# Two sequences' q and k loaded as three consecutive tokens per partition in two parts instead of six in one

## The chip, the cores and the metric

The kernel runs on one core of a Trainium2 chip. The metric is the device time of one execution in microseconds (us), the median of several runs. All runs compared here are of the state "fast". The engines are named as the profile names them: PE (TensorE matmuls), PEld (its weight loads), DVE (VectorE), ACT (ScalarE), POOL (GpSimd) and SP (SyncE, which here only issues transfers).

## The reference

Eight sequences of 576 tokens, eight heads of 64, go through causal attention with a window of 128 and a linear distance bias (ALiBi). A block with LayerNorm, a 512 to 2048 to 512 ReLU MLP and a residual follows. Cut to what matters:

```python
scores = q @ k.T / sqrt(64) + bias;  attn = softmax(where(0 <= i - j < 128, scores, -1e9))
x = (attn @ v) as (8, 576, 512);     xn = (x - mean) / sqrt(var + 1e-6) * g_ln
out = x + relu(xn @ w_ch1) @ w_ch2
```

q, k and v are drawn with a standard deviation of 0.1. The scaled products q·k therefore have a spread of about 0.1 x 0.1 x 8 / 8 = 0.01, and the bias decides the softmax almost alone.

## The kernel before

The kernel walks through head pairs of one sequence. For each pair it loads q and k, casts them to fp16, transposes them on PE into a PSUM tile `ptr` (features on partitions, tokens along the row), and copies that tile to SBUF (`qt`, `kt`) for the score matmuls. Sequences 2 to 7 are loaded in runs of 256 bytes (64 floats). Sequences 0 and 1 are needed early, so partition p takes the six consecutive tokens 6p to 6p+5, which makes runs of 1536 bytes. The price is paid after the transposes. Transpose t yields the tokens t, 6+t, 12+t, ..., so the copy out of PSUM must write every sixth fp16 element, 12 bytes apart:

```python
NWIDE = 2; QI = 6; QP = S // QI                       # 96 partitions, 6 tokens each
# load, sequences 0 and 1
out=t[0:QP, :].rearrange("p (h x) -> p h x", h=2),
in_=s.rearrange("h (p i) d -> p h (i d)", i=QI),
...                                                   # cast to c16
for t in range(QI):
    nc.tensor.transpose(ptr[:, t * QP : t * QP + QP], c16[:, t, :, :]..., iden[0:QP, 0:QP])
nc.vector.tensor_copy(                                # line 272
    out=dst[:, 0:S].rearrange("c (p i) -> c i p", i=QI),
    in_=ptr[:, :].rearrange("c (i p) -> c i p", i=QI))
...                                                   # sequences 2 to 7: line 287, dense
nc.vector.tensor_copy(out=dst[:, 0:S], in_=ptr[:, :])
```

After the score matmuls ACT takes the exponential, and DVE multiplies `probs` with the decay mask: line 338 with `mband`, line 347 with `m2g`, a rearranged copy of it. During sequence 0, POOL builds `m2g` and does casts:

```python
def mask_pair(hp):                                    # called once per pair of sequence 0
    nc.gpsimd.tensor_copy(m2g[:, hs, 0:192], mband[:, hs, 0:192])
    nc.gpsimd.tensor_copy(m2g[:, hs, 192:256], mband[:, hs, 0:64])
    nc.gpsimd.tensor_copy(m2g[:, hs, 256:512], mband[:, hs, :])
```

Sequence 0's attention runs alone. Sequence 1's attention runs beside the MLP of the first 512 rows, and so on.

The softmax here doesn't subtract the row's maximum and nothing guards it: scores larger than these inputs give would overflow.

## Time and profile before

| | before |
|---|---|
| median of three runs (range) | 411.57 us (410.92 to 412.39) |
| PE busy, 12 to 41 us (sequence 0) | 11.62 of 29 us |
| PE busy, 110 to 400 us | 286.71 of 290 us |
| one copy of line 272 (12-byte writes), recorded, means of its groups | 2.07 to 2.19 us |
| one copy of line 287 (dense), same 128x576 | 0.458 us |

The first lines are from the profile page of the kernel before: PE's busy share and the granted PE clock in 40 equal slices of the span, in tenths (9 is 90% or more).

```profile
PE   1344497775499999999999999999999999999996
...
PEclk9999998988599999999999999999999999999999
```

The stretches of the same trace have the columns: stretch in us, its length, busy time of PE, PEld, DVE, ACT and POOL (instructions in brackets), granted clock, DMA share, GB/s.

```profile
12.00:41.00 29.00, 11.62 (x138) 8.60 (x138) 21.45 (x30) 9.55 (x15) 12.12 (x20) 1.00 1.15 197
...
62.00:72.00 10.00, 7.55 (x42) 2.72 (x39) 6.21 (x6) 3.84 (x5) 2.14 (x3) 0.83 0.80 181
...
82.00:92.00 10.00, 7.48 (x53) 3.09 (x50) 6.08 (x8) 2.05 (x2) 0.00 (x0) 0.83 0.00 0
...
110.00:400.00 290.00, 286.71 (x2038) 135.91 (x2038) 176.44 (x418) 125.83 (x206) 0.00 (x0) 0.99 0.36 91
```

From 110 us on PE is busy 286.71 of 290 us, so only work before that point can be shortened by this change. Before it PE has gaps.

The groups of instructions of the first 115 us, by shape (line, engine, operation, out<-in, shape, count | busy us, mean ns | idle before), show one group of strided copies and one dense copy:

```profile
L272 DVE COPY kt_115<-ptr 128x576 f16<-128x576 f16 x3 | 6.6, 2193 | 0.0
...
L287 DVE COPY qt_113<-ptr 128x576 f16<-128x576 f16 x1 | 0.5, 458 | 3.0 <-PE ptr L282 3.0
```

The DVE timeline (start us, us, engine, line, operation, out<-in, count, and in brackets the idle time before and its releaser) of sequence 0's first two head pairs, cut to copies and mask multiplies:

```profile
6.69 2.07 DVE L272 COPY qt_111<-ptr 128x576 f16<-128x576 f16 x1 [4.16 <-PE ptr L267]
8.48 2.19 DVE L272 COPY kt_114<-ptr 128x576 f16<-128x576 f16 x1
12.43 0.82 DVE L338 TENSOR_TENSOR probs<-probs,mband 128x1024 f16<-128x1024 f16 x1 [1.76 <-ACT probs L333]
13.48 0.69 DVE L347 TENSOR_TENSOR probs<-probs,m2g 128x1024 f16<-128x1024 f16 x1 [0.22 <-ACT probs L329]
...
21.68 2.07 DVE L272 COPY qt_113<-ptr 128x576 f16<-128x576 f16 x1 [1.72 <-PE ptr L267]
23.47 0.80 DVE L338 TENSOR_TENSOR probs<-probs,mband 128x1024 f16<-128x1024 f16 x1
```

The q and k copies at 6.69 and 8.48 us are back to back and start 1.79 us apart. The q copy at 21.68 us belongs to the next pair. The mask multiply at 23.47 us stands behind it on DVE: its input, an exponential on ACT, was finished at 21.68 us (20.66 + 1.02), but it starts only when the copy is through.

The PE timeline of sequence 1 shows what the copies cost there. In brackets is PE's idle time before the score matmuls:

```profile
66.28 0.49 PE L320 MATMUL sc<-qt_112,kt_115 64*128 64x256 f16 x4 [2.45 <-DVE kt_115 L272]
...
77.83 0.39 PE L320 MATMUL sc<-qt_113,kt_116 64*128 64x256 f16 x4 [2.52 <-DVE kt_116 L272]
...
87.36 0.61 PE L320 MATMUL sc<-qt_111,kt_114 64*128 64x256 f16 x4 [2.52 <-DVE kt_114 L272]
...
88.30 1.91 PE L483 MATMUL pm_771<-w2sb,ht 128*128 128x512 f16 x4
...
98.55 0.39 PE L320 MATMUL sc<-qt_112,kt_115 64*128 64x256 f16 x4 [2.18 <-DVE kt_115 L272]
```

PE waits 2.45, 2.52, 2.52 and 2.18 us for the k copies. The four matmuls of 512 columns at 88.30 us, after one of these waits, take 1.91 us together; the granted clock from 88.30 to 90.20 us is 0.50 (and again 0.50 from 66.71 to 68.96 us, after the first wait).

### The profile page before, as it was taken

How to read it: one execution, taken by the hardware profiler on the slowest of the kernel's cores; microseconds unless marked ns; L12 is line 12 of the kernel's file. 1: busy time of each engine (PE TensorE's matmuls, PEld its weight loads, DVE VectorE, ACT ScalarE, POOL GpSimd, SP SyncE). 2: the span in 40 equal slices, each digit the busy share in tenths (PEclk: the TensorE clock that was granted, in tenths of full speed). 3: DMA queues.
4: the chain of work that ended last, by engine and by line, in shares of the span. 5: the costliest groups of instructions: out<-in, count | busy, mean ns of one | idle time of the engine just before them, and what ended most of it. 6: DMA issues, size and time to landing. Idle time of an engine off the chain costs nothing.

```text
span 410.8 us, 6580 instructions
## 1 busy us (share of the span) xinstructions
PE 352.6 (86%) x2544; PEld 170.6 (42%) x2544; DVE 254.8 (62%) x555; ACT 158.2 (39%) x257; POOL 28.4 (7%) x54
## 2 busy tenths in 40 slices
PE   1344497775499999999999999999999999999996
PEld 0232243323344454445444444444444444444442
DVE  5686936669656776677678576857685768222211
ACT  2341353111356235614651564165326533530510
POOL 4750432000000000000000000000000000000000
PEclk9999998988599999999999999999999999999999
DMA  9999997503624543457345335644421004002002
GB/s 205 199 204 197 235 174 177 114 0 122 149 59 109 128 129 99 94 145 197 85 106 146 115 85 122 152 138 111 113 81 53 0 2 133 29 0 78 26 27 77
DMA packets 110271, 45.30 MB, mean 110 GB/s; under 512 B 97440, under 2 KB 105120, under 8 KB 110240
## 3 DMA queue, kind: packets, MB, share of 16 engines
q1 hardware_dynamic: 105664, 40.36, 40.3%
q0 software_dynamic: 4224, 4.19, 6.4%
q8 instruction: 20, 0.33, 0.3%
q10 hardware_dynamic: 352, 0.33, 0.3%
q14 instruction: 11, 0.09, 0.1%
HBM read 37.26 MB, written 9.44 MB: 114 GB/s over the span
## 4 chain that ended last, share of the span: by engine, by line
PE 57%; DVE 22%; ACT 9%; issue 7%; DMA 3%; SPq 1%; DVEq 0%; ACTq 0%
PE pm L497 21%; PE pm L464 20%; ACT probs L333 6%; DVE probs L347 5%; PE ptr L282 4%; PE ppv L360 3%; PE pxt L425 3%; PE sc L320 2%; ACT ht L472 2%; PE ppv L369 2%; DVE kt_114 L272 2%; DVE st L399 1%; DVE qt_112 L272 1%; DMA v_1_106<-in_v_dram 1%; DMA iden<-iden 1%
## 5 line engine op out<-in xcount | busy, mean ns | idle before, releaser
L497 PE MATMUL pm<-w2sb,ht 128*128 128x512 f16 x512 | 123.4, 379 | 0.0
L472 ACT ACTIVATE ht<-pm 128x512 f16<-128x512 f32 x108 | 64.6, 598 | 83.7 <-PE pm L464 83.7
L333 ACT ACTIVATE probs<-sc 128x1024 f16<-128x1024 f32 x60 | 61.4, 1023 | 90.6 <-PE sc L320 90.6
L464 PEld LDWEIGHTS <-w1sb 128*128 128x128 f16 x576 | 48.8, 99 | 52.5 <-issue 7.5
L497 PEld LDWEIGHTS <-ht 128*128 128x128 f16 x512 | 45.4, 98 | 45.2 <-issue 1.3
L338 DVE TENSOR_TENSOR probs<-probs,mband 128x1024 f16<-128x1024 f16 x32 | 22.5, 703 | 41.5 <-ACT probs L333 41.5
L474 DVE TENSOR_SCALAR ht<-pm 128x512 f16<-128x512 f32 x36 | 24.8, 688 | 33.9 <-PE pm L464 33.9
L360 PEld LDWEIGHTS <-probs 128*128 128x128 f16 x320 | 25.2, 102 | 37.0 <-DVE probs L347 15.5
L360 PE MATMUL ppv<-vx_131,probs 128*128 128x65 f16 x160 | 16.4, 206 | 10.0 <-DVE probs L338 7.9
L347 DVE TENSOR_TENSOR probs<-probs,m2g 128x1024 f16<-128x1024 f16 x32 | 21.9, 685 | 4.2 <-ACT probs L333 3.6
L402 ACT ACTIVATE lv<-mv,eps_t 128x4 f32<-128x4 f32 (+1 forms) x16 | 4.5, 296 | 51.1 <-DVE mv L400 50.3
L425 PE MATMUL pxt<-iden,xs 128*128 128x128 f16 x128 | 13.3, 241 | 12.2 <-DVE xs L415 11.7
L447 DVE TENSOR_TENSOR o_tile<-pm,xp_3206 128x512 f32<-128x512 f32 x9 | 6.2, 692 | 24.2 <-PE pm L497 24.2
L369 PEld LDWEIGHTS <-probs 128*128 128x128 f16 x256 | 20.8, 103 | 0.0
L464 PE MATMUL pm<-xt_488,w1sb 128*128 128x512 f16 x64 | 17.5, 431 | 0.2 <-ACT xt_488 L433 0.2
L464 PE MATMUL pm<-xt_524,w1sb 128*128 128x512 f16 x64 | 17.6, 396 | 0.0
L320 PE MATMUL sc<-qt_112,kt_115 64*128 64x256 f16 (+2 forms) x104 | 8.8, 264 | 10.1 <-DVE kt_115 L272 8.6
L377 DVE RECIPROCAL rec<-ppv 128x5 f32<-128x5 f32 x64 | 12.0, 197 | 8.8 <-PE ppv L369 6.3
L425 PEld LDWEIGHTS <-xs 128*128 128x128 f16 x128 | 9.5, 107 | 18.9 <-DVE xs L415 14.5
L360 PE MATMUL ppv<-vx_132,probs 128*128 128x65 f16 x160 | 15.2, 197 | 2.4 <-DVE probs L347 0.9
L464 PE MATMUL pm<-xt_2633,w1sb 128*128 128x512 f16 x64 | 16.6, 381 | 0.0
L464 PE MATMUL pm<-xt_1059,w1sb 128*128 128x512 f16 x64 | 16.6, 381 | 0.0
(331 smaller groups left out, 486.3 us busy)
## 6 DMA issues: line engine op xcount, KB each, us to landing
out_dram<-o_tile SPq DMA_DIRECT2D x36, 256.0 KB, 2.0
v_0_105<-in_v_dram SPq DMA_DIRECT2D x16, 128.0 KB, 2.8
v_1_106<-in_v_dram SPq DMA_DIRECT2D x16, 128.0 KB, 2.7
v_2_107<-in_v_dram SPq DMA_DIRECT2D x16, 128.0 KB, 2.6
v_3_108<-in_v_dram SPq DMA_DIRECT2D x16, 128.0 KB, 2.7
w1sb<-in_moe_w_ch_dram POOLq DMA_DIRECT2D x4, 512.0 KB, 8.1
w2sb<-in_moe_w_ch_dram POOLq DMA_DIRECT2D x4, 512.0 KB, 14.0
q_0_97<-in_q_dram SPq DMA_DIRECT2D x12, 128.0 KB, 2.7
```

The costliest lines, as they stand in the source:

```text
L282: nc.tensor.transpose(ptr[:, sb * P : sb * P + n], c16[0:n, sb, :, :].rearrange("p h d -> p (h d)"), iden[0:n, 0:n],)
L320: nc.tensor.matmul(halves[g][:, OFF[j] : OFF[j] + NQ[j]], kt[r0 : r0 + D, j * P : j * P + P], qt[r0 : r0 + D, j * P : j * P + NQ[j]], star ...
L333: nc.scalar.activation(out=probs[:, :, :], in_=sc[:, :, :], func=AF.Exp, scale=inv_sqrt_d)
L338: new_mask = nc.vector.tensor_tensor(out=view, in0=view, in1=mband[:, 2 * hp : 2 * hp + 2, :] .unsqueeze(2) .broadcast_to([P, 2, 2, 2 * P] ...
L347: nc.vector.tensor_tensor(out=probs[:, :, :], in0=probs[:, :, :], in1=m2g[:, 2 * hp : 2 * hp + 2, :], op=ALU.mult,)
L360: nc.tensor.matmul(ppv[:, qb, :], pr[GRP[qb]][:, g, OFF[qb] : OFF[qb] + P], vx[:, qb, h, 0 : D + 1], start=True, stop=(qb == 0),)
L369: nc.tensor.matmul(ppv[:, qb, :], pr[GRP[j]][:, g, OFF[j] + P : OFF[j] + 2 * P], vx[:, j, h, 0 : D + 1], start=False, stop=True,)
L425: nc.tensor.transpose(pxt[:, kb, :], xs[:, kb * P : kb * P + P], iden[:, :])
L464: nc.tensor.matmul(pm[:, :], w1sb[:, kb, fb * P : fb * P + P], xt[:, kb, :], start=(kb == 0), stop=(kb == NKB - 1),)
L472: nc.scalar.activation(out=ht[:, fb, :], in_=pm[:, :], func=AF.Relu)
L474: gates["scale"] = nc.vector.tensor_scalar(out=ht[:, fb, :], in0=pm[:, :], scalar1=0.0, scalar2=None, op0=ALU.max)
L497: nc.tensor.matmul(pm[:, :], ht[:, fb, tb * P : tb * P + P], w2sb[:, fb, :], start=(fb == 0), stop=(fb == NFB - 1),)
```

## The change

The intent is to halve the write step. A partition now takes three consecutive tokens in each of two halves of the sequence: tokens 3p to 3p+2 and 288+3p to 288+3p+2. The copy then writes every third fp16 element, 6 bytes apart. The price is that runs of the load shrink from 1536 to 768 bytes. The number and order of all instructions stay the same on every engine (PE 2544, DVE 555, ACT 257, POOL 54). The core of the diff:

```diff
-    QI = 6
-    QP = S // QI
+    QI = 3
+    QP = 96
+    QJ = S // (QI * QP)
 ...
-                    out=t[0:QP, :].rearrange("p (h x) -> p h x", h=2),
-                    in_=s.rearrange("h (p i) d -> p h (i d)", i=QI),
+                    out=t[0:QP, :].rearrange("p (n x) -> p n x", n=2 * QJ),
+                    in_=s.rearrange("h (j p i) d -> p (h j) (i d)", p=QP, i=QI),
 ...
-                    for t in range(QI):
+                    for t in range(QJ * QI):
 ...
-                        out=dst[:, 0:S].rearrange("c (p i) -> c i p", i=QI),
-                        in_=ptr[:, :].rearrange("c (i p) -> c i p", i=QI),
+                        out=dst[:, 0:S].rearrange("c (j p i) -> c j i p", i=QI, j=QJ),
+                        in_=ptr[:, :].rearrange("c (j i p) -> c j i p", i=QI, j=QJ),
```

Line numbers shift by two: the copy is line 270 after the change, the mask multiplies are lines 336 and 345.

More of the change, by code (lines that the diff above doesn't have):

```diff
@@ L83 @@
     NWIDE = 2
-    QI = 6
-    QP = S // QI
+    QI = 3
+    QP = 96
+    QJ = S // (QI * QP)
     NSTG = 4
     NQT = 3
-    q32 = [persist.tile([P, 2 * QI * D], FP32, tag=f"q32{i}", name=f"q32_{i}") for i in range(NSTG)]
-    k32 = [persist.tile([P, 2 * QI * D], FP32, tag=f"k32{i}", name=f"k32_{i}") for i in range(NSTG)]
+    q32 = [persist.tile([P, 2 * QJ * QI * D], FP32, tag=f"q32{i}", name=f"q32_{i}") for i in range(NSTG)]
+    k32 = [persist.tile([P, 2 * QJ * QI * D], FP32, tag=f"k32{i}", name=f"k32_{i}") for i in range(NSTG)]
     v32 = [persist.tile([P, NFULL, 2, D], FP32, tag=f"v32{i}", name=f"v32_{i}") for i in range(NSTG)]
@@ L106, in gated @@
         return d
-    def wide_view(t):
-        return t[0:QP, :].rearrange("p (h i d) -> p h i d", h=2, i=QI)
     def block_view(t):
@@ L257, in attn_gen @@
                 dst = ring[(b * HPAIRS + hp) % NQT]
-                s16 = st16_pool.tile([P, QI, 2, D], FP16, tag=f"{nm}16")
+                s16 = st16_pool.tile([P, QJ * QI, 2, D], FP16, tag=f"{nm}16")
                 if b < NWIDE:
-                    src = wide_view(stg).rearrange("p h i d -> p i h d")
                     c16 = s16[0:QP, :, :, :]
+                    src = stg[0:QP, :].rearrange("p (h t d) -> p t h d", h=2, d=D)
                     if b == 0 and nm == "q":
```

## The prediction

> **What bounds the kernel now.** 411.57 us on one core. The table of stretches shows two regimes. From 110 us to the end PE is busy 287 of 290 us, and the change touches nothing there. Before that PE is often idle: busy 11.6 of 29 us in 12 to 41 us (sequence 0), 22.5 of 30 us in 62 to 92 us (sequence 1 beside the first MLP chunk). There the chain of waits runs through the 16 copies of line 272, which bring the transposed q and k from PSUM to SBUF with writes 12 bytes apart. In the groups of instructions one lasts 2.07 to 2.19 us; back to back they start 1.79 us apart (6.69 and 8.48 us in the DVE timeline). The unstrided copy of the same 128x576 (line 287) takes 0.458 us.
>
> **What changes.** No instruction is added, removed or reordered. Copies: the write step goes from 12 to 6 bytes, the read stays dense. The q and k loads of two sequences keep their bytes, but contiguous runs halve from 1536 to 768 bytes. Casts, transposes and matmuls keep their shapes.
>
> **Cost of a copy after.** [...] A cost proportional to bytes spanned gives 0.9 us. No trace yet decides. I take 0.9 us of pitch (about 1.2 us recorded): 0.9 us saved per copy.
>
> **How much lies on the chain.** Sequence 0: all eight. Pairs 0 and 1 have both copies serially before the score matmuls; in pairs 2 and 3 the q copy sits in DVE order ahead of a mask multiply that was ready (it starts at 23.47, ready about 21.7), the k copy ahead of the scores. 8 x 0.9 = 7 us. Sequence 1: PE waits 2.45, 2.52, 2.52 and 2.18 us at the score matmuls for the k copy; two copies save 1.8 us per pair, inside these waits: 7 us. After two of these waits matmuls run at half clock (four at 88.3 us take 1.91 instead of 0.86); shorter waits may save up to 1 us more. Against it: shorter DMA runs at the start, where DMA share is 0.97, an estimate of 0.3 us before the first transposes. Later loads have several us of slack (second sequence's first casts end at 47 us, transposes come at 61 us). The gain isn't given back: what follows is PE-bound with unchanged work.
>
> **Prediction.** 397.5 us, 8 in 10 between 392.5 and 405. Faster by over 2%: 0.78; within 2%: 0.21; slower: 0.01.
>
> **What would show it.** Line 272 copies about 1.2 us recorded, pitch 0.9; the last normalising multiply of sequence 0 (ends 41.0 us) about 7 us earlier; PE's waits for k copies in sequence 1 under 1 us; the PE-bound stretch shifted by about 14 us; first transposes at 6.0 to 6.4 us.
>
> **What would make it wrong.** Partial writes paid per element: no gain. [...] Smaller runs delaying first loads or weights. A lower granted clock once PE idles less.

411.57 less 7 (sequence 0) less 7 (sequence 1) is 397.6 us, and with up to 1 us for the clock and 0.3 us against it the forecast was put at 397.5. The 0.9 us of pitch is an estimate, half of the measured 1.79 us for half the step. The 0.3 us for shorter DMA runs was the estimate; no trace shows it.

## The result

The changed kernel took 397.71 us (median of four runs, 395.57 to 398.36) against 411.79 us before (median of four). The ratio is 0.9651, with a 95% interval of 0.961 to 0.9691. Ratios here are the mean time of one kernel's fast runs over that of the other's of the same rounds, so not quite the ratio of the medians quoted.

The same two lines of the page of the kernel after. PE fills up earlier, and the 8s of the clock are gone (mean granted clock 0.983 to 0.987 in the four runs):

```profile
PE   1443698964999999999999999999999999999995
...
PEclk9999999995999999999999999999999999999999
```

All copies of line 270, by tile (count: shortest/median/longest ns, first and last start; shapes), are at half of the old duration:

```profile
L270 DVE COPY qt_111<-ptr x3: 1115/1115/1125, 7.0 to 73.9; 128x576 f16<-128x576 f16 x3
...
L270 DVE COPY kt_115<-ptr x3: 1100/1101/1108, 17.1 to 82.8; 128x576 f16<-128x576 f16 x3
```

PE in sequence 1, to be held against the five lines of before:

```profile
60.09 0.39 PE L318 MATMUL sc<-qt_112,kt_115 64*128 64x256 f16 x4 [0.54 <-DVE kt_115 L270]
...
68.38 0.39 PE L318 MATMUL sc<-qt_113,kt_116 64*128 64x256 f16 x4 [0.62 <-DVE kt_116 L270]
...
76.00 0.39 PE L318 MATMUL sc<-qt_111,kt_114 64*128 64x256 f16 x4 [0.62 <-DVE kt_114 L270]
...
76.55 1.03 PE L481 MATMUL pm_771<-w2sb,ht 128*128 128x512 f16 x4
...
83.93 0.39 PE L318 MATMUL sc<-qt_112,kt_115 64*128 64x256 f16 x4 [0.27 <-DVE kt_115 L270]
```

The waits for k copies fell from 2.45, 2.52, 2.52 and 2.18 us to 0.54, 0.62, 0.62 and 0.27 us. The four matmuls after the third wait take 1.03 us.

Sequence 0 holds a surprise. This is the timeline of all engines, cut to DVE and POOL around the mask multiplies of the first two pairs:

```profile
10.76 0.82 POOL L263 CAST s_256<-k_1_102 96x768 f16<-96x768 f32 x1 [1.58 <-DMA k_1_102<-in_k_dram]
10.81 2.55 DVE L336 TENSOR_TENSOR probs<-probs,mband 128x1024 f16<-128x1024 f16 x1 [1.76 <-ACT probs L331]
11.53 0.50 POOL L192 COPY m2g<-mband 128x384 f16<-128x384 f16 x1
...
12.21 0.61 POOL L194 COPY m2g<-mband 128x512 f16<-128x512 f16 x1
12.77 1.06 POOL L291 CAST vx_131<-v_1_106 128x512 f16<-128x512 f32 x1
...
13.29 1.09 DVE L345 TENSOR_TENSOR probs<-probs,m2g 128x1024 f16<-128x1024 f16 x1
...
19.30 3.10 POOL L208 DMA_DIRECT2D w1sb<-in_moe_w_ch_dram  x4 [1.83 <-DMA k_3_104<-in_k_dram]
...
20.94 1.68 DVE L336 TENSOR_TENSOR probs<-probs,mband 128x1024 f16<-128x1024 f16 x1
...
22.54 1.86 DVE L345 TENSOR_TENSOR probs<-probs,m2g 128x1024 f16<-128x1024 f16 x1
```

The multiplies, 0.67 to 0.82 us long before, now last 2.55, 1.09, 1.68 and 1.86 us. POOL copies, casts and the issue of weight transfers lie beside them.

To see where time went, the trace can be cut at three events: the start of the first q copy, the first LayerNorm statistic of sequence 0, and that of sequence 1. Times in us, each from a profiled execution; "after, again" is a second profile of the same changed kernel.

| stage | before | after | after, again |
|---|---|---|---|
| start to first q copy | 6.69 | 6.98 | 7.65 |
| first q copy to statistics of sequence 0 | 34.36 | 30.75 | 27.79 |
| from there to statistics of sequence 1 | 63.12 | 51.61 | 51.57 |
| from there to the end | 306.63 | 306.76 | 307.59 |
| span | 410.8 | 396.1 | 394.6 |

Sequence 0 gained 3.6 us in one execution and 6.6 in the other. Sequence 1 gained 11.5 us in both. After it nothing was given back in the first; in the second the rest took about 1 us longer than before.

### The profile page after: what moved, and what is told of

Read it like the earlier page. It is cut to its first block, busy times and chain, and to the rows that moved or that the text cites. A ratio compares the mean times of both kernels' runs of the same rounds, so it can differ in the third digit from the quotient of the medians.

```text
span 396.1 us, 6580 instructions
## 1 busy us (share of the span) xinstructions
PE 349.4 (88%) x2544; PEld 169.7 (43%) x2544; DVE 242.9 (61%) x555; ACT 158.0 (40%) x257; POOL 29.6 (7%) x54
## 4 chain that ended last, share of the span: by engine, by line
PE 59%; DVE 20%; ACT 8%; issue 7%; DMA 4%; DVEq 0%; SPq 0%; ACTq 0%
PE pm L495 22%; PE pm L462 20%; DVE probs L345 5%; ACT probs L331 5%; PE ptr L280 4%; PE pxt L423 3%; PE ppv L358 3%; PE sc L318 2%; DMA v_1_106<-in_v_dram 2%; ACT ht L470 2%; PE ppv L367 2%; DVE st L397 2%; DMA iden<-iden 1%; DVE kt_114 L270 1%; DVE qt_112 L270 1%
## 5 line engine op out<-in xcount | busy, mean ns | idle before, releaser
L495 PEld LDWEIGHTS <-ht 128*128 128x128 f16 x512 | 45.4, 97 | 45.2 <-issue 1.3
L336 DVE TENSOR_TENSOR probs<-probs,mband 128x1024 f16<-128x1024 f16 x32 | 25.0, 780 | 41.2 <-ACT probs L331 41.2
L358 PEld LDWEIGHTS <-probs 128*128 128x128 f16 x320 | 24.7, 101 | 39.2 <-DVE probs L345 16.7
L345 DVE TENSOR_TENSOR probs<-probs,m2g 128x1024 f16<-128x1024 f16 x32 | 23.4, 732 | 2.8 <-ACT probs L331 2.5
L367 PEld LDWEIGHTS <-probs 128*128 128x128 f16 x256 | 20.5, 102 | 0.0
L462 PE MATMUL pm<-xt_524,w1sb 128*128 128x512 f16 x64 | 17.6, 396 | 0.0
L462 PE MATMUL pm<-xt_1593,w1sb 128*128 128x512 f16 x64 | 16.6, 381 | 0.0
L462 PE MATMUL pm<-xt_2633,w1sb 128*128 128x512 f16 x64 | 16.6, 381 | 0.0
L462 PE MATMUL pm<-xt_3150,w1sb 128*128 128x512 f16 x64 | 16.6, 381 | 0.0
L462 PE MATMUL pm<-xt_2107,w1sb 128*128 128x512 f16 x64 | 16.6, 381 | 0.0
```

The costliest lines, as they stand in the source:

```text
L336: new_mask = nc.vector.tensor_tensor(out=view, in0=view, in1=mband[:, 2 * hp : 2 * hp + 2, :] .unsqueeze(2) .broadcast_to([P, 2, 2, 2 * P] ...
L345: nc.vector.tensor_tensor(out=probs[:, :, :], in0=probs[:, :, :], in1=m2g[:, 2 * hp : 2 * hp + 2, :], op=ALU.mult,)
L358: nc.tensor.matmul(ppv[:, qb, :], pr[GRP[qb]][:, g, OFF[qb] : OFF[qb] + P], vx[:, qb, h, 0 : D + 1], start=True, stop=(qb == 0),)
L367: nc.tensor.matmul(ppv[:, qb, :], pr[GRP[j]][:, g, OFF[j] + P : OFF[j] + 2 * P], vx[:, j, h, 0 : D + 1], start=False, stop=True,)
L462: nc.tensor.matmul(pm[:, :], w1sb[:, kb, fb * P : fb * P + P], xt[:, kb, :], start=(kb == 0), stop=(kb == NKB - 1),)
L495: nc.tensor.matmul(pm[:, :], ht[:, fb, tb * P : tb * P + P], w2sb[:, fb, :], start=(fb == 0), stop=(fb == NFB - 1),)
```

## The experiments

Theory: the write step is the whole gain; the copies' place on the chain in both sequences gives it its size; part of sequence 0's gain is taken by collisions between DVE's two-input multiplies and POOL. Rivals: the new loads have a share; the multiplies were stretched by something else; the cost of a copy follows another rule than lines touched.

### Loads alone and writes alone

The first kernel is the changed one with the old copy pattern, the second is the kernel before with the new copy pattern:

```diff
 # e1_loads_alone, in the changed kernel
-  out=dst[:, 0:S].rearrange("c (j p i) -> c j i p", i=QI, j=QJ), in_=ptr[...] "c (j i p) -> c j i p"
+  out=dst[:, 0:S].rearrange("c (p i) -> c i p", i=QI * QJ),      in_=ptr[...] "c (i p) -> c i p"
 # e2_writes_alone, in the kernel before
-  out=dst[:, 0:S].rearrange("c (p i) -> c i p", i=QI),           in_=ptr[...] "c (i p) -> c i p"
+  out=dst[:, 0:S].rearrange("c (j p i) -> c j i p", i=3, j=2),   in_=ptr[...] "c (j i p) -> c j i p"
```

> The changed kernel with the old 12-byte write step in its copies (wrong token order on purpose, so the output is wrong; the work is the same). Theory (the write step is the whole gain, the 768-byte loads only cost some 0.3 us at the start): 411.5 to 412.5 us, copies 2.07 to 2.19 us each, first transposes at about 6.3 us. Rival (the new loads themselves move the time): 2 us or more away from 411.8.

> The kernel before with its 1536-byte loads, and the new 6-byte write step in the copies (wrong token order on purpose, wrong output). Theory (the write step is the whole gain): 396.5 to 398 us, copies about 1.1 us, first transposes at 6.0 us. Rival (the loads carry part of the gain): above 399 us.

Both put tokens in a wrong order. Both were nevertheless accepted by the comparison with the reference. A likely reason is the spread of 0.01 of the scaled q·k products: the comparison hardly sees which q meets which k. For these two runs it does not matter; for any other edit of these copies it means that the token mapping must be checked by reading.

Loads alone: 411.72 us (411.54 to 413.24), ratio 1.001, interval 0.9973 to 1.0048. Writes alone: 396.32 us (394.70 to 396.68), ratio 0.9631, interval 0.9593 to 0.9669. The write step alone gives the whole gain; the rival falls. The stage from the first q copy to the statistics of sequence 0 took 28.99 us in its profile, a gain of 5.4 us, between the two of the changed kernel. The loads' cost is not separable from zero. The estimate of 0.3 us for the start can be neither shown nor refuted: the first q copy starts between 6.98 and 7.65 us in the six profiles with 768-byte loads and between 6.59 and 7.76 us in the seven with 1536-byte loads for the first sequence (the copy-timing kernel below is not counted).

### What a write step costs

> The kernel before plus, at its very end with all else idle, 48 more VectorE copies of a 128x576 fp16 PSUM tile into SBUF: dense reads with write steps of 2, 4, 6, 8, 10, 12, 14, 16, 20, 24 bytes, three of each, then dense writes with PSUM reads stepping 576, 384, 288, 192, 128, 96 bytes (2, 3, 4, 6, 9, 12 streams). By start-to-start pitch. The two measured points are 1.79 us at 12 bytes and 0.96 at 6. Line theory (cost per 16-byte line touched[...]): 0.66 us at 4 bytes, 1.2 at 8, 1.5 at 10, 1.8 at 12, 2.1 at 14, 2.4 at 16, and flat at 2.4 for 20 and 24. Byte-proportional theory: the same up to 16 and then on to 3.5 at 24. 8-byte-pair theory[...]: about 1.8 at 8 and flat from there. Reads in steps: if a PSUM read step is as dear as an SBUF write step, 1.8 us or more; if it is nearly free, 0.66 to 0.8 us.

```diff
+    pp = att_psum.tile([P, S], FP16, ...)                       # 128x576 in PSUM, filled by transposes
+    scr = w1sb[:, :, :].rearrange("p k f -> p (k f)")           # no longer needed at the end
+    for step in 1, 2, 3, 4, 5, 6, 7, 8, 10, 12 elements, three times each:
+        nc.vector.tensor_copy(out=<every step-th element of scr>, in_=pp[:, :])
+    for i in 2, 3, 4, 6, 9, 12, three times each:
+        nc.vector.tensor_copy(out=scr[:, 0:S] "c (p i) -> c p i", in_=pp "c (i p) -> c p i")
```

One execution, its state unknown, with the added copies on an otherwise idle core (480.06 us in all, so not a time to compare). Per line of the kernel (count: shortest/median/longest ns): write steps of 2, 4, 6, 8, 12, 16 and 24 bytes, then a dense write whose PSUM read alternates between twelve streams 96 bytes apart:

```profile
L539 DVE COPY w1sb<-pprobe x3: 447/457/458, 407.8 to 408.8; 128x576 f16<-128x576 f16 x3
...
L542 DVE COPY w1sb<-pprobe x3: 796/797/797, 409.3 to 410.9; 128x576 f16<-128x576 f16 x3
...
L545 DVE COPY w1sb<-pprobe x3: 1114/1115/1115, 411.8 to 414.1; 128x576 f16<-128x576 f16 x3
...
L548 DVE COPY w1sb<-pprobe x3: 1430/1431/1431, 415.2 to 418.2; 128x576 f16<-128x576 f16 x3
...
L554 DVE COPY w1sb<-pprobe x3: 2066/2066/2066, 425.0 to 429.2; 128x576 f16<-128x576 f16 x3
...
L560 DVE COPY w1sb<-pprobe x3: 2701/2701/2701, 438.5 to 444.0; 128x576 f16<-128x576 f16 x3
...
L566 DVE COPY w1sb<-pprobe x3: 2676/2676/2678, 454.9 to 460.3; 128x576 f16<-128x576 f16 x3
...
L584 DVE COPY w1sb<-pprobe x3: 757/757/757, 474.9 to 476.5; 128x576 f16<-128x576 f16 x3
```

Recorded durations from 4 to 16 bytes lie on a straight line, 0.16 us plus 0.159 us per byte of step, and stay flat at 2.68 to 2.70 us from 16 to 24 bytes. That is the line theory's shape: a fixed price per 16-byte line touched, (2.70 - 0.16) us / 576 = about 4.4 ns per line. The dense write, eight elements per line, lies close to it (0.48 us by this rule, 0.457 measured). Twelve bytes touch three lines with four elements, 6 bytes three lines with eight, hence the halving. So 12 bytes should take 0.16 + 3/4 x 2.54 = 2.06 us, and 6 bytes 0.16 + 3/8 x 2.54 = 1.11; measured were 2.07 and 1.11. The byte-proportional theory falls at 20 and 24 bytes, the 8-byte-pair theory at 8 bytes (1.43 us where it wanted about as much as at 12, 2.07). Pitches (from start to start) came out 0.2 to 0.3 us above those expected, at 16 bytes 2.74 instead of 2.4. Here each copy overwrites the one before, so it may have waited for its end; that was not tested.

The last line is the more useful find: with a dense write, a stepped read from PSUM costs 0.30 us more than the dense copy (0.757 against 0.457 us), however far it jumps. In all six cases, 2 to 12 streams and 96 to 576 bytes apart, the three copies took 2.34 us together.

### Stepped reads and dense writes

> The kernel before with its 1536-byte loads; the copies go through the tokens in order, so they write densely in SBUF and read the PSUM tile in steps of 192 bytes (right result). If stepped PSUM reads are nearly free: copies 0.7 to 0.9 us recorded, total 392.5 to 396 us. If a stepped PSUM read costs as much as the stepped write did: copies of about 2 us, total 410 to 413.

```diff
 # e6_densewrite, in the kernel before (loads of 1536 bytes kept)
-  out=dst[:, 0:S].rearrange("c (p i) -> c i p", i=QI), in_=ptr[...] "c (i p) -> c i p"
+  out=dst[:, 0:S].rearrange("c (p i) -> c p i", i=QI), in_=ptr[...] "c (i p) -> c p i"
```

The same tokens go to the same places, but in token order, so the jumping is done by the read. 394.44 us (392.54 to 395.21), ratio 0.9559, interval 0.9521 to 0.9597, right result. The copies took 0.75 us, as expected. This beats the change on both of its terms: a cheaper copy, with the long load runs. But each copy got 0.36 us cheaper than in the change, which is 5.8 us over 16 copies, and only about 3 us came out. A DVE line of late sequence 1 shows one place where the rest went:

```profile
78.00 0.75 DVE L272 COPY kt<-ptr 128x576 f16<-128x576 f16 x1
...
82.18 0.69 DVE L447 TENSOR_TENSOR o_tile<-pm,xp 128x512 f32<-128x512 f32 x1 [2.24 <-DMA out_dram<-o_tile]
```

The fourth residual add of the first MLP chunk (82.18 us) waited 2.24 us for an output transfer to free one of the three output buffers, and held up the mask multiply behind it. The profile after has no such wait. A fourth output buffer would be the next thing to try. It was not run.

### Sequence 1 alone

> Three-token parts and 6-byte writes for sequence 1 only; sequence 0 as before (12 bytes, 1536-byte loads). Reading of the two traces (sequence 1 gained about 10.5 of the 14.7 us: waits 7.6 us and the rest matmul clock): 400.5 to 402 us. The prediction's split (7 us here, up to 1 more for the clock): 403.5 to 405 us.

```diff
 # e3_seq1, in the changed kernel: load and copy
-  three tokens in two parts for b < 2
+  three tokens in two parts for b == 1; six tokens in one part, 12-byte writes for b == 0
```

402.08 us (400.43 to 402.84), ratio 0.9757, interval 0.9721 to 0.9793, beside 412.75 us. The gain is about 10 us, at the edge of the first expectation and clearly more than the 7 to 8 us of the prediction's split. The stage from statistics to statistics took 51.22 us, and in it the waits for the k copies are those of the kernel after. By the ratios, some 4 to 5 us are then left to sequence 0, between its two profiled gains of 3.6 and 6.6 us (this ratio against the two measured for the changed kernel, so only an estimate).

### Taking POOL's copies away from the multiplies

> The changed kernel, with the doubled mask table (12 GpSimd copies) built only after sequence 0's last mask multiply; sequence 0's second multiply is split in three that read the original mask. Theory (the multiplies that stretched to 2.55, 1.68, 1.86 us in sequence 0 waited for GpSimd's SBUF reads): the first multiply of pair 0 falls below 1.9 us (one cast still overlaps), the second multiplies no longer stretch, sequence 0's last normalising multiply ends 1 to 2.5 us earlier than 37.7, and the total is 395 to 397 us although the split adds an estimated 0.2 us per pair. Rival (DMA traffic or ScalarE stretched them): first multiplies stay at 2.5 and 1.7 us, the total rises to 398 to 399 by the split.

> Control: the same late mask table and split multiply in the kernel before. Theory (collisions with GpSimd are nearly absent there: the multiplies took 0.67 to 0.82 us): the split costs and nothing is gained, 411.5 to 413 us. Rival (the edit helps for another reason): 410 us or less.

```diff
 # e4_latemask (in the changed kernel), e5_before_latemask (in the kernel before)
-                mask_pair(hp)                                   # during sequence 0
+    for hp in range(HPAIRS): mask_pair(hp)                      # emitted after sequence 0
+    add_manual_dep(<first of the 12 copies>, <last mask multiply of sequence 0>)
-  one multiply of probs with m2g (sequence 0)
+  three multiplies of its pieces with mband (sequence 0)
```

e4 took 398.78 us (397.43 to 400.08), ratio 0.9688; e5 took 411.65 us (410.92 to 412.48), ratio 1.0001. The edit failed to do what it was meant to do: only one of the twelve copies was tied to the last multiply, and the scheduler moved the eleven others back to their early places. So e4 tests nothing about their absence. Its profile still has stretched multiplies (2.62 us for the three pieces of pair 0, 1.29 and 2.27 us in pair 1). In e5 the same edit in the kernel before cost nothing that can be seen.

> The changed kernel, with all 12 GpSimd copies of the doubled mask table now truly held back until sequence 0's last mask multiply (in e4_latemask only one of them waited, the rest ran early as before); sequence 0's second multiply in three pieces. Theory (GpSimd reads of SBUF stretch the two-input multiplies): pair 0's and pair 1's multiplies near 0.7 to 1.3 us apart from one overlapping cast each, sequence 0's last normalising multiply ends 1 to 2.5 us before 37.7, total 395.5 to 397 us, about 0.6 us of split cost included. Rival (DMA or ScalarE stretch them): a multiply of over 1.6 us stays in pair 0 and pair 1, total 398 to 399.

```diff
 # e8_gatedmask: as e4, but each of the 12 copies waits for sequence 0's last mask multiply
+        for c0, c1 in ((0, 192), (192, 256), (256, 512)):
+            d = nc.gpsimd.tensor_copy(m2g[:, hs, c0:c1], mband[:, hs, 0 : c1 - c0])
+            tc.add_manual_dep(d.ins, gates["mask"].ins.name, SYNC, ...)
```

395.76 us (395.31 to 396.46), ratio 0.9599, interval 0.9568 to 0.963. In this profile, without POOL's copies, the multiplies of pairs 0 and 1 are short again; where one cast starts second, it is now the cast that is long:

```profile
11.25 0.69 DVE L335 TENSOR_TENSOR probs<-probs,mband 128x1024 f16<-128x1024 f16 x1 [1.76 <-ACT probs L330]
11.45 1.18 POOL L263 CAST s<-k 96x768 f16<-96x768 f32 x1 [1.87 <-DMA k<-in_k_dram]
...
12.23 1.08 DVE L345 TENSOR_TENSOR probs<-probs,mband 128x384 f16<-128x384 f16 x3 [0.28 <-ACT probs L326]
...
19.86 0.67 DVE L335 TENSOR_TENSOR probs<-probs,mband 128x1024 f16<-128x1024 f16 x1
...
20.45 0.81 DVE L345 TENSOR_TENSOR probs<-probs,mband 128x384 f16<-128x384 f16 x3
```

From the first q copy to the statistics of sequence 0 it took 27.50 us instead of 30.75. The three pieces took 0.81 us together in pair 1, one multiply 0.67 us there in the kernel before (24.19 us): 0.14 us for the split, of which 0.2 per pair was expected. So far this fits the theory. The kernels were then repeated side by side, to see whether this counts in the total:

> The changed kernel once more, on the same chip as the others of this call, for a direct comparison: 395.5 to 398.5 us, ratio 0.963 to 0.968; if the stretched multiplies are there again (their place varies), sequence 0's last normalising multiply ends between 36 and 38.5 us.

> The held-back mask table once more beside the changed kernel itself: 1 to 2.5 us below after_again in the median if the collisions cost what the traces show; no difference if they only moved the time.

The changed kernel: 396.39 us (395.54 to 399.23), ratio 0.9626, interval 0.9595 to 0.9656. With held-back copies: 396.14 us (394.48 to 397.27), ratio 0.9605, interval 0.9576 to 0.9635. That is 0.25 us between the medians: the expected 1 to 2.5 us did not come. The profiles give two reasons. First, the collisions differ from execution to execution. This time the changed kernel met few of them although its copies were in place (DVE timeline):

```profile
11.48 0.69 DVE L336 TENSOR_TENSOR probs<-probs,mband 128x1024 f16<-128x1024 f16 x1 [1.76 <-ACT probs L331]
...
12.53 1.33 DVE L345 TENSOR_TENSOR probs<-probs,m2g 128x1024 f16<-128x1024 f16 x1 [0.35 <-ACT probs L327]
...
20.42 0.67 DVE L336 TENSOR_TENSOR probs<-probs,mband 128x1024 f16<-128x1024 f16 x1
```

and its first stage took 27.79 us, less than the 28.33 us of e8_again. Second, e8 gave time back: its stage from statistics to statistics took 53.22 us (53.30 in e8_again) against 51.57 and 51.61. The MLP's first matmuls ran slow for longer. In groups of instructions of two stretches of e8 (42.4 to 45.4 us, then 50 to 53 us) the same matmul has mean durations of

```profile
L469 PE MATMUL pm<-xt,w1sb 128*128 128x512 f16 x8 | 3.6, 625 | 0.0
```
```profile
L469 PE MATMUL pm<-xt,w1sb 128*128 128x512 f16 x15 | 3.4, 379 | 0.0
```

In steps of 2 us from the first of these matmuls on, 5, 6, 9 and 11 of them were running in e8, and 6, 11, 11 and 11 in the second profile of the changed kernel. From that first matmul to sequence 1's first q copy e8 took 13.36 us (13.34 in e8_again), the two profiles of the changed kernel 12.73 and 12.02. The rest of what was given back lies later and was not traced. Why PE stayed slow for longer is open: the granted clock reads 1.00 in all of these steps, and no run here isolates a cause.

### Trying for more

> A try for a better version: e6_densewrite (six tokens per partition, dense writes, stepped PSUM reads) with the mask table held back as in e8_gatedmask. If the two gains are independent (e6 took 0.3 us off each copy, e8 removed the stretched multiplies): 392 to 393.5 us, ratio 0.950 to 0.955. If the dense copies only shift other waits: 394 to 395, as e6.

> e9_dense_gated, with sequence 0's four large v casts moved from GpSimd to ScalarE, so that fewer GpSimd reads can meet a mask multiply. Theory (collisions still cost up to 1 us): 0.3 to 1 us below e9. Rival (the casts then stand in ScalarE's order ahead of an exponential): equal to e9 or up to 1.5 us above.

```diff
 # e9_dense_gated = e6_densewrite + e8_gatedmask;  e10_dense_gated_vact = e9 +
-  vc = nc.gpsimd.tensor_copy(out=vx[...], in_=v32[i])             # sequence 0
+  vc = nc.scalar.activation(out=vx[...], in_=v32[i], func=Copy)
```

e9: 394.31 us (393.64 to 394.48), ratio 0.956, interval 0.9534 to 0.9586. e10: 393.60 us (392.09 to 394.63), ratio 0.9542, interval 0.9513 to 0.957. Neither differs clearly from e6_densewrite (0.9559). e10 lies 0.7 us below e9 in the median, as its theory expected, but the intervals overlap. e9's expected independence failed, as the last sentence of its expectation foresaw: its profile has the wait for an output buffer too (2.30 us). In all three the stage from statistics to statistics is longer than the 51.6 us of the changed kernel: 52.92 us in e6, 53.01 in e9 and 52.56 in e10. Part of what sequence 0 wins is given back there, as in e8. The simplest of the three, e6_densewrite, is the version to keep: one copy's loop order changed, and both kernels beaten.

## Why the prediction was right

The total was predicted as 397.5 us and measured as 397.71. The terms, one by one:

- **The bound.** "What follows is PE-bound with unchanged work" held: from the statistics of sequence 1 to the end both kernels took 306.6 to 306.8 us in the first two profiles, and the changed kernel 307.6 in the third.
- **The copy.** Predicted 0.9 us of pitch (from start to start) and 1.2 us recorded; measured 0.96 (6.98 to 7.94 us) and 1.11. The rule it took, a cost proportional to bytes spanned, was near for a step from 12 to 6 bytes; the copy timings replace it with a price of about 4.4 ns per 16-byte line, since 20 and 24 bytes cost no more than 16 (2.68 to 2.70 us).
- **Sequence 0.** Predicted 7 us for eight copies; 8 x (1.79 - 0.96) is 6.6 us. One execution of the changed kernel shows exactly that (34.36 to 27.79 us), the other only 3.6, and e2's 5.4. The step "in pairs 2 and 3 the q copy sits in DVE order ahead of a mask multiply that was ready" was right about the chain, but the prediction did not ask what the earlier multiplies would meet. Before, POOL was nearly done when DVE reached them (pair 0: POOL's copies ended at 12.15 us, the first multiply started at 12.43). Now its copies, casts and transfer issues lie in the same microseconds, and in the profiled execution the four multiplies of pairs 0 and 1 took 4.5 us more than 0.67 to 0.69 each.
- **Sequence 1.** Predicted 7 us, plus up to 1 for the clock; measured 11.5. The waits for k copies shrank by 9.67 - 2.05 = 7.6 us, as predicted. The clock's term was mis-sized. In the stretches 62 to 72 and 82 to 92 us the granted clock was 0.83 before; in the same stretches of the sequences' work after (62 to 82 us) it was 1.00. The four waits divide the score matmuls' starts into three intervals: 11.55, 9.53 and 11.19 us before (from 66.28, 77.83 and 87.36 us), 8.29, 7.62 and 7.93 after. The shorter wait at the end of each explains 1.9 us. The second shrank by just that; the two that open with slow matmuls shrank by 1.36 and 1.35 us more, together 2.7 us. In e1 and e5, which also write 12 bytes apart, only one of the four waits was followed by slow matmuls (granted clock 0.66 from 86 to 91 us in e1 and from 66 to 71 us in e5, 1.00 in the other stretches of 5 us between 61 and 96 us), and the stage took 60.97 and 61.35 us instead of 63.12. So the clock is worth 1 to 3 us by execution. Another 0.9 us came between statistics and MLP (49.44 - 41.05 against 45.23 - 37.73 us), where before the LayerNorm scalings that stood beside POOL casts took longer (0.91 against 0.40 us for one of the same shape). With the 7.6 us of waits and the 2.7 of the clock, that accounts for 11.2 of the 11.5 us.
- **Loads.** "An estimate of 0.3 us" stayed within noise.

The two deviations, about 3.4 us less in sequence 0 and 3.5 to 4.5 us more in sequence 1, cancelled in the profiled execution. The close hit of the total is partly that luck. The range was right because it allowed for a copy cheaper or dearer than 0.9 us of pitch, and the one number that decided, 0.96, fell close to that.

On the collisions: that a two-input multiply on DVE and a POOL instruction beside it hold each other up, the one that starts second waiting for the first, is the reading of single overlaps. It fits where copies and casts are concerned: in the kernel after, the multiply that starts 0.05 us after a cast lasts 2.55 us, to 13.36 us. The cast ended at 11.58 us, so the three copies queued behind it, which ran to 12.82 us, seem to have gone first too. In e8 the multiply starts first and takes 0.69 us, and the cast 1.18 instead of 0.82. That the copies did it is argued from such overlaps. The removal does not show it: without them e8's multiplies were short, but in the second profile of the changed kernel, with the copies in place, those of pairs 0 and 1 took only 0.69, 1.33, 0.67 and 0.68 us. Not explained is the 1.68 us multiply at 20.94 us, beside which POOL only issues weight transfers: in other executions multiplies beside the same issues took 0.67 us (20.42 us in the second profile of the changed kernel) or, three pieces together, 1.86 us (20.16 us in e8_again). No pattern was found in this, and it stays open.

## What to carry to other kernels

When an eviction must permute, let the PSUM read jump and keep the SBUF write dense: on this chip the same 128x576 copy took 0.76 us with stepped reads, 1.11 with 6-byte and 2.07 with 12-byte writes. Shortening one engine's work moves the next instructions into other neighbours, so ask of each freed instruction what POOL is doing at its new time, and check a gain over several executions. Short PE waits can cost more than their length, because the matmuls after them may run at half clock: in the kernel before they did after two of the four waits (granted clock 0.50, four matmuls in 1.91 us after a wait of 2.52 us; at 1.00 they took 1.03 us after one of 0.62). Shortening such waits then pays more than their sum.
